# A folded block DFT, summed neighbour spectra and a list-scheduled program in a gated long-convolution and mixer kernel

## The chip, the cores and the metric

The kernel runs on one core of a Trainium2 chip. The metric is device time in microseconds (us) of that core, from the first instruction to the last. All data are bf16, with float32 sums in PSUM. A run counts as fast or slow by its time: a run that is over 1.5% above the fastest of the same kernel is called slow and is left out of the ratios.

Engine names in the profile: PE is TensorE's matmuls, PEld its weight loads, DVE is VectorE, ACT is ScalarE, POOL is GpSimd, SP is SyncE, which here only issues DMAs.

## The reference, cut to what matters

There are two branches over one sequence of 2048 rows of 640 channels, and a gate that mixes them. Branch A multiplies a 4-tap filter of `k` by `v`, convolves the product along the sequence with a filter as long as the sequence (`ssm_k`), and multiplies by `q`. Branch B is a mixer and an MLP with two layer norms.

```python
x = A_q                                            # (1, 2048, 640)
g = _sigmoid((x * gate_w).sum(-1, keepdims=True))
# branch A
for t in range(ks):                                # ks = 4
    k_shift = k_shift + k_pad[:, t:t + S, :] * shift_k[:, ks - 1 - t][None, None, :]
kv = k_shift * v
...
y_f = kv_f * kf_f[None, :, :, :]                   # FFTs of 4096: a causal convolution of 2048
y = y + kv * ssm_D[None, None, :]
a = q * y
# branch B
h = _gelu(_layernorm(x, axis=-1) @ w1)
# four groups of channels of h, shifted by +1, -1, +2, -2 rows
hs = jnp.concatenate([g0, g1, g2, g3], axis=-1) @ w2
x1 = x + hs
h2 = _gelu(_layernorm(x1, axis=-1) @ w3) @ w4      # w3 is 640x1536, w4 is 1536x640
b = x1 + h2
out = g * a + (1 - g) * b
```

I call the four products with `w1`, `w2`, `w3` and `w4` the first to fourth matmul, and the two layer norms LN1 and LN2.

## The kernel before

The convolution is done in four blocks of 512 rows by DFTs of 1024 points, as matmuls. The spectra of `kv` (per block) and of the filter (per block) are multiplied on VectorE, block by block, and summed. The frequencies and channels are cut into eight *units* (four groups of 128 frequencies times two halves of the channels). The inverse DFT is again matmuls; an output row needs the product spectra of its own block and of the block before it.

A helper records every operation with the names of what it reads and writes, and derives the waits. Each engine issues its operations in the order in which the program recorded them:

```python
    def _add(self, op):
        eng = op.eng
        op.ordinal = len(self.per_eng[eng])
        ...
        self.per_eng[eng].append(op)
        self.ops.append(op)
        return op
```

The product `kv` takes four shifted loads of `k` and eight operations of 640 elements for each tile of 128 rows:

```python
        for j in range(4):
            r0 = t * 128 - j
            if r0 >= 0:
                P.dma("sp", kvin[s][j], A_k[0, r0:r0 + 128, :], w=[("kvin", s, j)])
            ...
```

The second matmul's residual is added by VectorE as it reads PSUM, and VectorE also takes LN2's statistics:

```python
    def mm2_s1(t):
        ...
        P.op("dve", lambda e: e.tensor_tensor(
            x1t.rearrange("p (b n) -> p b n", b=2), ps2, xr.rearrange("p (b n) -> p b n", b=2), ALU.add),
             r=[("bankB", 2 * pr), ("bankB", 2 * pr + 1), ("xrel", t % 3)], w=[("x1rot", t % 3)])
        ...
        ln_act(1, t, x1t, ("x1rot", t % 3))
```

A unit multiplies block spectra in 30 VectorE operations, which cover the real and the imaginary part one by one:

```python
            else:
                for (ri_h, kvsel, ytgt, opc, un) in ((0, "re", "re", ALU.add, False), (1, "im", "re", ALU.subtract, False),
                                                      (0, "im", "im", ALU.add, useN), (1, "re", "im", ALU.add, False)):
                    ...
                    P.op(eng, lambda e, pt=pt, kvap=kvap, ri_h=ri_h, a=a, nbb=nbb, un=un: e.tensor_tensor(
                        pt[:, 0:nbb, :], kvap, Hbc(ri_h, a, nbb, n=un), ALU.mult), r=rk, w=[pk])
                    yap = Yre(a) if ytgt == "re" else Yim(a)
                    P.op(eng, lambda e, pt=pt, yap=yap, nbb=nbb, opc=opc: e.tensor_tensor(yap, yap, pt[:, 0:nbb, :], opc),
                         r=[pk, ykey], w=[ykey])
```

The inverse reads two blocks for each output tile, and the stages come one after the other:

```python
            for fcx in range(8):
                mm.append((fcx, c, 128 * q))
                if c >= 1:
                    mm.append((fcx, c - 1, 512 + 128 * q))
...
    for u in range(8):
        alloc_slots(u)
        fwd_dft("h", u)
        fwd_dft("kv", u)
        pointwise(u)
        release_slots(u)
...
    for sc in range(4):
        emit_mm3(sc)
        emit_mm4(sc)
...
    pipeline([inv_s0, inv_s1, inv_s2], NT)
```

## Time and profile before

Three runs took 500.69, 501.24 and 503.26 us, median 501.24. The profiled run had a span of 500.8 us.

| engine | busy us | share of the span |
|---|---|---|
| TensorE | 307.9 | 61% |
| VectorE | 270.7 | 54% |
| ScalarE | 177.2 | 35% |
| GpSimd | 28.6 | 6% |

No engine is near its limit over the whole span. The overview rows of the page show why: each character is one fortieth of the span (12.5 us), a digit is the busy share in tenths, PEclk is the clock that TensorE was granted in tenths, and DMA is the busy share of the 16 DMA engines. The trace has clock records from 117.0 us on only; the nines of PEclk before that stand for no record.

```profile
PE   1100000004993468999136750399899999999996
...
DVE  1666773872017767799999999667102020232122
...
PEclk9999999999799956999759975599999999999999
DMA  6399999980004564660000000002301010132221
```

Read the rows from left to right. First DMA is at 9 and TensorE is empty; then VectorE is at 9 while TensorE is partly empty; at the end TensorE is at 9 and VectorE is at 0 to 3. The same in numbers, from the view that sums the busy time of each engine over stretches. The first numbers are the stretch and its length; then come the busy times of PE, PEld, DVE, ACT and POOL with their instruction counts, the granted clock, the DMA share and GB/s.

```profile
0.00:125.00 125.00, 13.99 (x122) 7.24 (x123) 73.41 (x222) 56.25 (x155) 13.32 (x25) 1.00 0.86 196
125.00:145.00 20.00, 19.04 (x77) 8.26 (x79) 0.00 (x0) 15.87 (x29) 0.00 (x0) 0.86 0.00 0
145.00:206.00 61.00, 40.25 (x213) 21.64 (x211) 40.72 (x97) 8.33 (x16) 12.85 (x33) 0.83 0.48 119
206.00:346.00 140.00, 86.37 (x425) 43.72 (x425) 126.78 (x248) 53.72 (x101) 1.90 (x2) 0.80 0.10 33
346.00:435.00 89.00, 86.77 (x528) 51.76 (x532) 13.17 (x15) 30.38 (x49) 0.56 (x1) 1.00 0.16 52
435.00:501.00 66.00, 61.52 (x453) 44.09 (x451) 16.66 (x33) 12.69 (x16) 0.00 (x0) 0.99 0.24 75
```

The fourth row is the units: VectorE is busy 126.78 of 140 us, and TensorE works beside it at a clock of 0.80. The fifth is the third and fourth matmul, 86.77 of 89 us on TensorE with VectorE almost free. These are two long stages with different engines at their limit, and they run in turn. The third row, the second matmul, has neither engine full: the chain of waits shows there a loop of 3.67 us per tile (the residual add, two statistics, GpSimd's inverse root, the normalisation).

Two groups of instructions matter below, the inverse (L905) and the second matmul's residual add (L653). After the count come the busy time in us, the mean of one in ns, and the idle time of the engine before the group with what ended it.

```profile
L905 PE MATMUL PA<-arena 128*128 128x320 bf16 x448 | 61.0, 299 | 0.0
...
L653 DVE TENSOR_TENSOR arena<-PB,arena 128x640 bf16<-128x640 f32 x16 | 13.1, 818 | 23.0 <-PE PB L644 23.0
```

The residual add takes 818 ns on VectorE, and before it VectorE waits for TensorE, 23.0 us in all: it is a link of the loop, not a side job. A matmul of 320 columns shows 299 ns from start to end, but they overlap: 61.0 us for 448 is 136 ns each. The Trainium skill, page "TensorE: Matmul & The Clock Gate", section "Back-to-back issue gap", gives N/2.4 + 2.5 ns as the gap of an isolated matmul on a warm array, 135.8 ns for N = 320, and says that this over-counts for large N in a sustained stream, about 131 ns for N = 512. In the streams of this trace the median from one start to the next is 136 ns for 320 columns and 216 ns for 512: the formula (215.8 ns for 512) fits here, and the lower figure for a stream doesn't. Cadences like this one, not the mean durations, are what a count of matmuls is to be multiplied by.

### The profile page before, as it was taken

Reading aid. Unit: us, or ns where it says so; the run is one execution under the profiler, and the core shown is the slowest. Engines: PE = TensorE matmul, PEld = TensorE weight load, DVE = VectorE, ACT = ScalarE, POOL = GpSimd, SP = SyncE. Lnnn points to the kernel's source line nnn. Section 1 sums busy time; section 2 is a strip of 40 time slices with the busy share of each in tenths; the row PEclk is TensorE's granted clock in tenths of the full one; section 3 lists DMA queues with packets and bytes.
Section 4 is the critical chain, followed back from the end, with each engine's and each line's share of the span. In section 5 each row is a group of like instructions: output and inputs, shape, how many; then the busy total and the mean of one; then the engine's idle time right before and its main releaser. Section 6 shows DMA issues by size and latency. Waiting matters only on the chain.

```text
span 500.8 us, 5285 instructions
## 1 busy us (share of the span) xinstructions
PE 307.9 (61%) x1809; PEld 176.7 (35%) x1819; DVE 270.7 (54%) x612; ACT 177.2 (35%) x363; POOL 28.6 (6%) x60
## 2 busy tenths in 40 slices
PE   1100000004993468999136750399899999999996
PEld 0000000001352234555013320146455565777774
DVE  1666773872017767799999999667102020232122
ACT  1754443426760001776023320272433425021111
POOL 3210110000001221200000000000000000000000
PEclk9999999999799956999759975599999999999999
DMA  6399999980004564660000000002301010132221
GB/s 199 107 228 246 259 279 170 257 200 7 0 27 118 132 144 107 178 241 1 0 1 0 0 1 0 1 0 67 154 12 42 1 54 0 41 106 79 81 80 52
DMA packets 59113, 46.00 MB, mean 92 GB/s; under 512 B 35136, under 2 KB 57662, under 8 KB 58830
## 3 DMA queue, kind: packets, MB, share of 16 engines
q1 hardware_dynamic: 36062, 31.46, 23.6%
q10 hardware_dynamic: 21152, 5.25, 7.2%
q0 software_dynamic: 1872, 8.96, 5.2%
q8 instruction: 14, 0.23, 0.2%
q14 instruction: 13, 0.11, 0.1%
HBM read 32.54 MB, written 5.24 MB: 75 GB/s over the span
## 4 chain that ended last, share of the span: by engine, by line
DVE 40%; PE 31%; DMA 14%; ACT 4%; issue 4%; POOL 3%; SPq 2%; DVEq 0%; ACTq 0%; POOLq 0%
PE PA L905 12%; DVE arena L802 9%; DVE arena L799 8%; PE PB L845 8%; DMA arena<-in_A_k_dram 8%; PE PA L821 5%; PE PB L600 4%; DMA arena<-x_scratch 3%; DVE arena L653 3%; DMA arena<-in_A_v_dram 2%; POOL arena L506 2%; SPq L125 2%; DVE arena L498 2%; DVE arena L499 2%; PE PA L740 1%
## 5 line engine op out<-in xcount | busy, mean ns | idle before, releaser
L740 PE MATMUL PA<-arena 128*128 128x512 bf16 (+1 forms) x384 | 78.6, 371 | 53.5 <-ACT arena L743 53.5
L743 ACT ACTIVATE arena<-PA 128x512 bf16<-128x512 f32 (+1 forms) x96 | 50.5, 526 | 131.3 <-PE PA L740 65.9
L740 PEld LDWEIGHTS PA<-arena 128*128 128x128 bf16 x384 | 39.8, 105 | 92.2 <-ACT arena L743 56.6
L571 PE MATMUL PA<-arena 128*128 128x1 bf16 x80 | 4.7, 169 | 93.7 <-DMA arena<-arena 93.7
L905 PE MATMUL PA<-arena 128*128 128x320 bf16 x448 | 61.0, 299 | 0.0
L855 DVE SCALAR_TENSOR_TENSOR arena<-PB,arena 128x640 bf16<-128x640 f32 x16 | 14.1, 884 | 76.5 <-PE PB L845 73.3
L821 PE MATMUL PA<-arena 128*128 128x512 bf16 x232 | 51.9, 379 | 2.3 <-ACT arena L587 1.9
L845 PE MATMUL PB<-arena 128*128 128x320 bf16 x384 | 52.8, 299 | 0.0
L905 PEld LDWEIGHTS PA<-arena 128*128 128x128 bf16 x448 | 43.8, 98 | 17.0
L802 DVE TENSOR_TENSOR arena<-arena 128x960 bf16<-128x960 bf16 (+2 forms) x96 | 47.2, 492 | 3.3
L799 DVE TENSOR_TENSOR arena<-arena 128x960 bf16<-128x960 bf16 (+2 forms) x96 | 46.6, 485 | 0.0
L644 PE MATMUL PB<-arena 128*128 128x320 bf16 x160 | 31.1, 354 | 20.8 <-DVE arena L653 20.2
L845 PEld LDWEIGHTS PB<-arena 128*128 128x128 bf16 x384 | 37.6, 98 | 15.2
L571 PEld LDWEIGHTS PA<-arena 128*128 128x128 bf16 x80 | 3.4, 107 | 95.1 <-DMA arena<-arena 95.1
L821 PEld LDWEIGHTS PA<-arena 128*128 128x128 bf16 x240 | 23.3, 98 | 30.3 <-ACT arena L587 3.4
L920 DVE TENSOR_TENSOR arena<-arena 128x640 bf16<-128x640 bf16 x16 | 7.9, 493 | 45.5 <-ACT arena L914 45.5
L914 ACT ACTIVATE arena<-PA,arena 128x640 bf16<-128x640 f32 x16 | 12.7, 793 | 54.7 <-PE PA L905 54.7
L587 ACT ACTIVATE arena<-PA 128x512 bf16<-128x512 f32 x48 | 27.0, 595 | 14.0 <-PE PA L821 14.0
L807 ACT ACTIVATE arena<-arena 128x640 bf16<-128x640 bf16 x16 | 12.8, 824 | 46.6 <-DMA arena<-x_scratch 46.6
L600 PE MATMUL PB<-arena 128*128 128x512 bf16 x98 | 25.4, 425 | 6.3 <-ACT arena L587 6.0
L644 PEld LDWEIGHTS PB<-arena 128*128 128x128 bf16 x160 | 16.6, 111 | 35.2 <-DVE arena L653 26.0
L475 ACT ACTIVATE arena<-arena 128x640 bf16<-128x640 bf16 x16 | 11.8, 735 | 42.3 <-issue 18.9
(82 smaller groups left out, 285.6 us busy)
## 6 DMA issues: line engine op xcount, KB each, us to landing
arena<-in_A_k_dram SPq DMA_DIRECT2D x61, 160.0 KB, 6.3
arena<-in_A_q_dram SPq DMA_DIRECT2D x48, 160.0 KB, 2.5
arena<-in_B_w_dram POOLq DMA_DIRECT2D x2, 1920.0 KB, 12.8
arena<-in_A_v_dram SPq DMA_DIRECT2D x16, 160.0 KB, 7.2
x_scratch<-arena SPq DMA_DIRECT2D x16, 160.0 KB, 1.8
arena<-x_scratch SPq DMA_DIRECT2D x16, 160.0 KB, 2.2
out_dram<-arena SPq DMA_DIRECT2D x16, 160.0 KB, 1.8
arena<-cG POOLq DMA_DIRECT2D x1, 2048.0 KB, 8.4
```

The source lines that it names most:

```text
L587: P.op("act", lambda e, dst=dst, src=src: e.activation(dst, src, ACTF.Gelu_apprx_tanh), r=[key_ps], w=wk)
L600: P.op("pe", lambda e, lhsT=lhsT, c=c, sc=sc, psb=psb: e.matmul(psb, lhsT, xT[:, c, sc * 512:(sc + 1) * 512], start=(c == 0), stop=(c == D ...
L644: P.op("pe", lambda e, lhsT=lhsT, ft=ft, hh=hh, bk=bks[hh]: e.matmul(bk[:, 0:320], lhsT, w2v[:, ft, hh * 320:(hh + 1) * 320], start=(ft == ...
L653: P.op("dve", lambda e: e.tensor_tensor(x1t.rearrange("p (b n) -> p b n", b=2), ps2, xr.rearrange("p (b n) -> p b n", b=2), ALU.add), r=[( ...
L740: P.op("pe", lambda e, psb=psb, tc=tc, q0=q0, rhs=rhs, ncol=ncol: e.matmul(psb[:, 0:ncol], Rv[:, tc, q0:q0 + 128], rhs, start=(tc == 0), s ...
L743: P.op("act", lambda e, psb=psb, dst=dst, bb0=bb0, bb1=bb1, dd0=dd0, dd1=dd1, nb_=nb_, ncol=ncol: e.activation(dst[:, bb0:bb1, dd0:dd1], p ...
L799: P.op(eng, lambda e, pt=pt, kvap=kvap, ri_h=ri_h, a=a, nbb=nbb, un=un: e.tensor_tensor(pt[:, 0:nbb, :], kvap, Hbc(ri_h, a, nbb, n=un), AL ...
L802: P.op(eng, lambda e, pt=pt, yap=yap, nbb=nbb, opc=opc: e.tensor_tensor(yap, yap, pt[:, 0:nbb, :], opc), r=[pk, ykey], w=[ykey])
L821: P.op("pe", lambda e, psb=psb, c=c, ft=ft: e.matmul(psb, w3v[:, c, ft * 128:(ft + 1) * 128], xT[:, c, sc * 512:(sc + 1) * 512], start=(c ...
L845: P.op("pe", lambda e, bk=bk, fcx=fcx, tt=tt, hh=hh: e.matmul(bk[:, 0:320], uT[:, fcx, (tt % 4) * 128:(tt % 4) * 128 + 128], w4v[:, fcx, h ...
L855: P.op("dve", lambda e: e.scalar_tensor_tensor(out=Bp[:, tt, :].rearrange("p (b n) -> p b n", b=2), in0=ps2, scalar=gcol(tt, 1), in1=x1r.r ...
L905: P.op("pe", lambda e, bk=bk, fcx=fcx, cc=cc, u0=u0, hh=hh, i=i, n_mm=n_mm: e.matmul(bk[:, 0:320], Gv[:, fcx, u0:u0 + 128], Yv[:, fcx, cc, ...
```

## The change

The intent is to give TensorE less to do, to give VectorE fewer and larger operations, and above all to let a scheduler put the stages beside each other. The parts are:

1. The DFT is taken at half-offset points, so that cosine and sine rows are even and odd about the middle of a block. A block is first folded (first half plus and minus the reversed second half), which halves the rows that the forward matmuls contract over.
2. The spectra of neighbouring blocks are summed per frequency before the units (`combine`), so that the inverse needs one block, not two.
3. A unit takes 19 operations, with the real and imaginary parts in one access pattern.
4. `kv` is made from one load with five rows per partition and one product of 5120 elements.
5. The residuals of second and fourth matmul are added on TensorE by a matmul with the identity; LN2's sums come from ScalarE's accumulator, and six small GpSimd operations make the mean and the inverse root of them.
6. The helper tracks hazards by memory region, and a list scheduler with constants for the cost of each operation orders the whole program for all engines before it is emitted. All transposes and nearly all loads and stores are issued by SyncE.

The diff, cut to its core (of some 850 lines on each side; `...` marks cuts):

```diff
-        self.per_eng[eng].append(op)
...
+    def schedule(self, bw=250.0, tbw=90.0, dlat=1900.0, lat=90.0, backlog=2500.0):
...
+                for i in cand[e]:
+                    st = max(f, ready[i])
+                    if ops[i].nbytes and not ops[i].tp:
+                        st = max(st, dfree - backlog)
+                    key = (st, -(ops[i].rank + ops[i].bias), i)
+                    if pick is None or key < pick:
+                        pick = key
...
-        P.op("dve", lambda e: e.tensor_tensor(pA, k0, SHK[0], ALU.mult), r=[("kvin", s, 0), ("SHK", 0)], w=[("ktmp", s, 0)])
...
+            P.dma(sp, kt, bass.AP(A_k.tensor, A_k.offset + (t0 - 3) * D, [[2 * D, 128], [D, 5], [1, D]]))
...
+        tt(kpr, win, SHK.unsqueeze(1).to_broadcast([128, 2, 4, 640]), ALU.mult)
...
+            tt(o, k[:, :, 0:256].rearrange("p b (n s) -> p b s n", s=2),
+               k[:, :, 511:255:-1].rearrange("p b (n s) -> p b s n", s=2), op)
...
-        P.op("dve", lambda e: e.tensor_tensor(
-            x1t.rearrange("p (b n) -> p b n", b=2), ps2, xr.rearrange("p (b n) -> p b n", b=2), ALU.add),
...
+            pairs.append((ident, xr[t % 3][:, hs]))
+            mm(pr[:, h, :], pairs)
+        act(x1[t % 3].rearrange("p (b n) -> p b n", b=2), pr, ACTF.Copy, accum=st[1, 0][:, t:t + 1])
+        act(xn2[t % 3], x1[t % 3], ACTF.Square, accum=st[1, 1][:, t:t + 1])
...
+        ts(s[2], s[0], 1.0 / D, None, ALU.mult, eng="pool")
+        ts(s[3], s[1], 1.0 / D, 1e-5, ALU.mult, ALU.add, eng="pool")
+        tt(s[4], s[2], s[2], ALU.mult, eng="pool")
+        tt(s[3], s[3], s[4], ALU.subtract, eng="pool")
...
+    def combine(b):
+        tt(XF[:, b, 0:2], XF[:, b, 0:2], XF[:, b - 1, 0:2], ALU.add)
+        tt(XF[:, b, 2:4], XF[:, b, 2:4], XF[:, b - 1, 2:4], ALU.subtract)
...
-                mm.append((fcx, c, 128 * q))
-                if c >= 1:
-                    mm.append((fcx, c - 1, 512 + 128 * q))
+        pairs = [(G[:, j, r, 128 * q:128 * (q + 1)], slots[order.index((j, hh))][:, r, c, :]) for j in range(4) for r in range(2)]
...
+    for i in range(4):
+        at(3, unit, i)
+    for sc in range(1, 4):
+        mm3(sc)
+        for i in range(4):
+            mm4(4 * sc + i)
+    for i in range(4, 8):
+        at(3, unit, i)
...
+    sched = P.schedule()
     with nc.Block() as block:
+        P.emit(block, sched)
```

## The prediction

It was written before the changed kernel ran.

> **What bounds the kernel now.** A row of stages (windows view). 0-125 us: loads, LN1, kv; DMA row at 9, VectorE 73 us busy. 145-206: second matmul in a VectorE loop of 3.67 us per tile (chain). 206-345: pointwise units; VectorE 99% full, 15.9 us for each of eight units of 30 operations; TensorE 40-60% busy at clock 0.6-0.8. 346-497: TensorE alone, 99% busy, clock 1.0: four rounds of third (8.8 us) and fourth matmul (13.05 us), then the inverse, 448 matmuls in 60.9 us. VectorE is mostly idle there.
>
> **What changes, in the trace's cadences** (TensorE 216 ns per 512 columns, 136 per 320).
> - TensorE: neighbour spectra are summed first, so the inverse is 256 matmuls, not 448 (-26 us); folding takes the forward from 256x512 plus 128x256 to 80x512 plus 144x320. Identity matmuls for residuals add 64x320 (+9). In all about 229 us at full clock, was 278.
> - VectorE: a unit keeps its 23,040 elements in 19 operations: about 13.7 us for 15.9. kv products become 32 large operations (46 us) plus folds (6); neighbour sums add 8.6. LN1 statistics come over from ScalarE (19); LN2 statistics and two residual adds leave (-50). The filter's folds read with step 2. The Trainium skill, "VectorE: DVE Perf Modes", section "What auto-detection actually checks", asks step 1 for the double rate, so I estimate 1.2 us for each of ten; nothing here shows it. Sum about 235 us, was 271.
> - ScalarE about 165 us, was 177. k is read 2.5 times in 6.4 KB rows, not 4 times in 1.3 KB rows.
> - Mainly order: the instruction order puts the units beside second, third and fourth matmul. Two stages that ran in turn (139 us VectorE, 150 us TensorE) overlap.
>
> **Sum.** Front: VectorE 99 us, DMA about as long, first tap rows at about 16 us: VectorE done with it at 120, the first MLP matmul at 105. Then TensorE has second 26, third 52, fourth 57, inverse 35 = 170 us. The second is bound by ScalarE (1.9 us per tile) and three buffers: 50 us including leftovers and the first third-matmul round. Then 131 us at 98%: 105 + 55 + 135 + tail 5 = 300. VectorE, 120 + 117 + stalls, ends just before; its order leaves 14 of 16 output pairs to the end, behind TensorE. I add a little for in-order stalls: the scheduler's constant for a 640-wide eviction, 660 ns, is under the measured 793.
>
> **Predicted 307 us**, 8 in 10 between 283 and 340. Faster by over 2%: 0.97; within: 0.02; slower: 0.01. All on the chain: about 25 front, 40 second matmul, 139 hidden, 25 inverse, less 35 of lost overlap.
>
> **What would show it.** Right: VectorE and TensorE each over 75% of the span; last 130 us TensorE at 9 and clock 1.0; a unit near 13.7 us; filter folds 1.1-1.3 us; the chain ends in 320-wide matmuls. Wrong: units still running after the last fourth matmul (then VectorE bounds); second-matmul tiles over 3 us.
>
> **What could make it wrong.** (1) LN2's six small GpSimd operations per tile now run beside two-input VectorE operations; the skill, "GPSIMD Engine Reference", section "1. Specifications", says the SBUF interfaces are shared and contend. Before, they took 222 and 568 ns with VectorE mostly waiting, so the trace cannot show it. A microsecond's wait each would make the second matmul 70 us: about 330. (2) Every transpose and load is on one in-order queue; one late producer blocks the rest. (3) Low clock in the front.

## The result, and the profile after

The changed kernel's median is 308.13 us (fast runs 306.93, 306.96 and 309.31; one run of 312.00 was slow; a fifth, 313.01, which the median leaves out, was slow too). In the same rounds the kernel before had a median of 500.97. The ratio is 0.615, with a 95% interval of 0.6086 to 0.6215. A ratio here is the mean time of one kernel's fast runs over that of the other's of the same rounds, so it is not quite the ratio of the medians quoted. The prediction was 307, so the total was right. The question for the experiments is whether it was right for the stated reasons.

The overview of the profiled run (a fast one, span 307.5 us), in slices of 7.7 us:

```profile
PE 249.3 (81%) x1526; PEld 144.0 (47%) x1526; DVE 229.0 (74%) x352; ACT 151.5 (49%) x289; POOL 87.8 (29%) x156
...
PE   0401949876797998747899599999999999999994
...
DVE  4489997989983934948879999999999991121343
...
PEclk9999997996999999887999799999999999999999
DMA  7978999978934047996633630004101311023342
```

TensorE and VectorE now have their nines in the same slices. The stretches, in the same columns as before:

```profile
0.00:100.00 100.00, 60.05 (x330) 26.91 (x331) 80.04 (x125) 55.12 (x102) 31.59 (x53) 0.95 0.87 226
100.00:179.00 79.00, 64.80 (x384) 37.92 (x383) 60.74 (x85) 47.66 (x104) 54.53 (x100) 0.94 0.61 165
179.00:257.00 78.00, 78.00 (x487) 46.94 (x486) 75.38 (x118) 29.06 (x49) 1.67 (x4) 1.00 0.17 43
257.00:308.00 51.00, 46.41 (x331) 32.18 (x329) 12.80 (x26) 19.61 (x35) 0.00 (x0) 0.98 0.28 78
```

In the third row both engines are over 95% busy at a clock of 1.00. This is what the change was for. The second row is not so good: TensorE 64.80 of 79 us, VectorE 60.74 of 79. The end of the chain of waits (start, duration, what) says what ended last:

```profile
178.80 124.63 PE PSall L506 x816
303.45 0.54 ACT arena L498
304.01 0.50 DVE arena L488
304.54 0.49 DVE arena L488
```

From 178.80 us on, 816 matmuls run without a break; one eviction, two VectorE operations and a store follow. The prediction had given the stages their own times, so they can be laid side by side. The first MLP matmul is over when its last 512-column matmul ends, ahead of a long run of 320-column ones; that is between 104.4 and 104.8 us.

| stage | predicted us | measured us |
|---|---|---|
| until the end of the first MLP matmul | 105 | about 104.6 |
| from there until TensorE runs without a break | 55 | 74.2 (178.8 - 104.6) |
| TensorE without a break | 135 | 124.6 |
| tail | 5 | 4.1 (307.5 - 303.4) |
| allowed for stalls in order | 7 | - |
| sum | 307 | 307.5 |

The middle stage was 19 us longer than its own line (the prediction's text has 50 us for it, its sum 55). The 7 us allowed for stalls and a last stage that was 10 us shorter made up for it. Two things shortened the last stage. The prediction's 135 us leave 4 us over its 131 us of matmuls for stalls, and there were none. And TensorE had done more of the later work: after 178.8 us, 170 matmuls of 512 columns and 646 of 320 remain, where the prediction's 131 us left 180 and 672 (three rounds of the third, all of the fourth, the inverse). The 10 and 26 that were pulled forward are 10 x 216 + 26 x 136 ns, 5.7 us.

How TensorE spent the middle stage (the same view, for this stretch alone):

```profile
104.60:178.80 74.20, 60.02 (x357) 35.80 (x356) 55.94 (x81) 44.81 (x100) 53.42 (x98) 0.93 0.65 176
```

It was busy for 60.0 us and idle for 14.2. So this stage would have been over its 55 us without a single wait. Its matmuls (286 of 320 columns and 70 of 512) come to 54 us at the cadences above, an estimate: second matmul 26, one round of the third 13, 9 for 67 forward-transform matmuls that were still left, and the 5.7 pulled forward. The other 6 us are slower matmuls, at a granted clock of 0.93 in the mean.

The VectorE groups that answer to the prediction's costs:

```profile
L488 DVE TENSOR_TENSOR arena<-arena 128x1280 bf16<-128x1280 bf16 x66 | 52.2, 817 | 5.2 <-PE PSall L506 4.0 <-ACT arena L498 0.9
L488 DVE TENSOR_TENSOR arena<-arena 128x2560 bf16<-128x2560 bf16 x28 | 41.6, 1485 | 3.2 <-ACT arena L498 3.0
...
L488 DVE TENSOR_TENSOR arena<-arena 128x5120 bf16<-128x5120 bf16 x8 | 22.6, 2824 | 3.1 <-ACT arena L498 2.8
...
L488 DVE TENSOR_TENSOR arena<-arena 128x1024 bf16<-128x1024 bf16 x10 | 11.8, 1210 | 0.0
```

The last line is the filter's folds with step 2: 1024 elements take 1210 ns, longer than 1280 elements with step 1 in the first line (817 ns). The prediction's estimate was 1.2 us.

### The profile page after: what moved, and what is told of

It reads as the page before. It is cut to its first block, busy times and chain, and to the rows that moved or that the text cites. A ratio compares the mean times of both kernels' runs of the same rounds, so it can differ in the third digit from the quotient of the medians.

```text
span 307.5 us, 4162 instructions
## 1 busy us (share of the span) xinstructions
PE 249.3 (81%) x1526; PEld 144.0 (47%) x1526; DVE 229.0 (74%) x352; ACT 151.5 (49%) x289; POOL 87.8 (29%) x156
## 3 DMA queue, kind: packets, MB, share of 16 engines
q1 hardware_dynamic: 52848, 35.40, 44.8%
## 4 chain that ended last, share of the span: by engine, by line
PE 52%; DVE 21%; DMA 11%; POOL 8%; ACT 4%; issue 3%; SPq 0%; ACTq 0%; POOLq 0%
PE PSall L506 51%; DVE arena L488 16%; DMA arena<-arena 8%; ACT arena L498 4%; POOL arena L652 3%; DVE arena L645 2%; POOL arena L488 2%; DMA arena<-in_A_shift_k_dram 2%; POOL arena L493 2%; DMA arena<-in_A_ssm_k_dram 2%; DVE arena L493 1%; POOL arena L661 1%; POOL arena L156 1%; DVE arena L646 1%; SPq L153 0%
## 5 line engine op out<-in xcount | busy, mean ns | idle before, releaser
L506 PE MATMUL PSall<-arena 128*128 128x320 bf16 (+3 forms) x1521 | 248.6, 323 | 46.2 <-ACT arena L498 14.2
L488 DVE TENSOR_TENSOR arena<-arena 128x640 bf16<-128x640 bf16 (+8 forms) x253 | 199.1, 836 | 51.0 <-ACT arena L498 43.4
L506 PEld LDWEIGHTS PSall<-arena 128*128 128x128 bf16 (+1 forms) x1521 | 143.5, 100 | 151.1 <-issue 32.5
L498 ACT ACTIVATE arena<-PSall 128x512 bf16<-128x512 f32 (+4 forms) x190 | 109.0, 613 | 85.6 <-PE PSall L506 68.5
L498 ACT ACTIVATE arena<-PSall,arena 128x320 bf16<-128x320 f32 (+1 forms) x48 | 29.5, 616 | 56.0 <-PE PSall L506 52.9
L493 POOL TENSOR_SCALAR arena<-arena 128x1 f32<-128x1 f32 (+2 forms) x44 | 23.0, 524 | 74.9 <-DVE arena L646 55.7
L493 DVE TENSOR_SCALAR arena<-arena 128x640 bf16<-128x640 bf16 (+2 forms) x36 | 15.5, 450 | 20.6 <-POOL arena L488 20.3
L488 POOL TENSOR_TENSOR arena<-arena 128x1 f32<-128x1 f32 (+2 forms) x60 | 24.4, 411 | 12.6 <-DVE arena L493 8.9
L645 DVE BATCH_NORM_STATS2 arena<-arena 128x6 f32<-128x320 bf16 x32 | 13.8, 473 | 3.0 <-DMA arena<-in_A_q_dram 3.0
L661 POOL TENSOR_TENSOR arena<-arena 128x1 f32<-128x1 f32 x16 | 12.9, 804 | 1.1
```

The lines of the kernel that those rows point to most:

```text
L488: P.op(eng, lambda e: e.tensor_tensor(o, a, b, op), [a, b], [o], dve_ns(o, [a, b], 2) if eng == "dve" else 250)
L493: P.op(eng, lambda e: e.tensor_scalar(o, a, s1, s2, op0=op0, **({} if op1 is None else {"op1": op1})), [a] + aps, [o], dve_ns(o, [a], 3) + ...
L498: P.op("act", lambda e: e.activation(o, a, f, bias=bias, scale=scale, **({"accum_out": accum} if accum is not None else {})), [a] + aps, [ ...
L506: fns.append(lambda e, l=l, r=r, i=i: e.matmul(o, l, r, start=(i == 0), stop=(i == len(pairs) - 1)))
L645: P.op("dve", lambda e, o=o, i=i: e.bn_stats(o, i), [i], [o], 420)
L661: P.op("pool", lambda e: e.tensor_tensor(s[5], s[3], neghalf[:, t0:t1], ALU.pow), [s[3], neghalf[:, t0:t1]], [s[5]], 600)
```

## The experiments

Twelve kernels ran, in four sets; within a set all ran on the same chip beside the kernel before, whose median was 500.9 to 502.1 us. Where the text says "order frozen", each engine keeps the changed kernel's order of instructions, so that only the stated edit differs. "The control" is the changed kernel once more.

| run | median us | lowest to highest | ratio to before (95%) |
|---|---|---|---|
| changed kernel | 308.13 | 306.93 to 312.00 | 0.6150 (0.6086 to 0.6215) |
| e11 control | 308.58 | 307.69 to 309.16 | 0.6167 (0.6126 to 0.6208) |
| e1 units before the second matmul | 415.69 | 414.99 to 417.58 | 0.8290 (0.8211 to 0.8369) |
| e2 recorded order | 605.54 | 604.49 to 607.00 | 1.2060 (1.1967 to 1.2152) |
| e3 two-block inverse | 337.39 | 334.86 to 339.44 | 0.6716 (0.6647 to 0.6785) |
| e4 forward matmuls twice | 324.68 | 324.22 to 324.85 | 0.6464 (0.6415 to 0.6512) |
| e5 LN2's small operations on VectorE | 314.70 | 312.26 to 317.62 | 0.6304 (0.6259 to 0.6349) |
| e6 more GpSimd operations in LN2 | 311.40 | 311.12 to 311.80 | 0.6219 (0.6204 to 0.6234) |
| e7 folds with step 1 | 310.43 | 309.24 to 311.32 | 0.6198 (0.6176 to 0.6219) |
| e8 fourth residual on VectorE | 306.25 | 304.12 to 308.03 | 0.6114 (0.6081 to 0.6147) |
| e9 four buffers in the second matmul | 319.36 | 317.51 to 320.39 | 0.6376 (0.6319 to 0.6433) |
| e10 folds with step 1 and less of k loaded | 307.11 | 303.36 to 311.54 | 0.6114 (0.6049 to 0.6179) |
| e12 less of w3 and w4 loaded | 307.21 | 305.92 to 310.41 | 0.6147 (0.6115 to 0.6178) |

All but e12 passed the comparison with the reference; e10 computes with missing rows of `k`, and the comparison's tolerance doesn't see it, presumably because the convolution's part of the output is small with these inputs (not tested). The medians of the changed kernel and its control differ by 0.45 us and their runs spread over 2 to 3 us, so I call nothing under 2 us a difference. Differences in the text below are taken from 308.4 us, the middle of these two medians. Medians and ranges count every run, slow ones too: 312.00 of the changed kernel, 317.62 of e5 and 311.54 of e10. The seven fast runs of changed kernel and control have a median of 308.27 us, so this matters for e5 and e10 only. (The ratio for e5 counts its slow run.)

### e1: is the gain the overlap?

The theory is that most of the gain is VectorE's units running beside second, third and fourth matmul. The edit tells the helper, falsely, that the first tile of the second matmul reads all unit outputs, so the units must come first; nothing is removed or added.

```diff
-            mm(pr[:, h, :], pairs)
+            mm(pr[:, h, :], pairs, after=list(slots[0:8]) if t == 0 else ())
...
+    for i in range(8):
+        at(3, unit, i)
     for t in range(12):
         mid(t)
```

> The changed kernel with one false dependence: the first group of the second matmul also waits for all eight pointwise units, so the units run before it instead of beside it (the units are recorded ahead of it). Result correct. Theory (the overlap of the units with the second, third and fourth matmul is the largest part of the gain): units from about 124 to 241 us, then second matmul about 40, then 131 and a tail of 5: 405 to 425 us, that is 100 or more lost. Rival (most of the gain is less work on each engine and the overlap is worth little because the engines slow each other down): under 345 us.

It took 415.69 us, 107 us more. The stretches show the stages in turn again, VectorE 114.72 of 122 us alone and then TensorE 118.84 of 123 us alone:

```profile
110.00:232.00 122.00, 12.50 (x62) 5.20 (x62) 114.72 (x171) 7.53 (x13) 4.26 (x8) 0.56 0.08 21
232.00:290.00 58.00, 52.30 (x321) 31.17 (x323) 7.79 (x19) 33.54 (x80) 25.75 (x100) 0.98 0.71 167
290.00:413.00 123.00, 118.84 (x775) 75.62 (x778) 15.75 (x32) 47.90 (x82) 0.00 (x0) 0.99 0.20 55
```

The theory holds, and so does its size: the prediction's "139 hidden, less 35 of lost overlap" is 104. One thing blurs the number: this kernel was scheduled anew, and the new order pushed the last five matmuls of the first MLP matmul behind the units (TensorE waited 97.86 us for a small VectorE copy that stood behind them, and then ran five 512-column matmuls, 2.3 us), so the 107 is not the overlap alone. A sign of the idle time is the clock row of the page, where TensorE is granted half its clock while the units run. The Trainium skill, page "TensorE: Matmul & The Clock Gate", section "What's actually happening", has the clock at half rate after idling, and here it stands at 5 tenths in the slices in which TensorE is idle:

```profile
PE   1136757888816000000000677999999999999996
...
PEclk9997999898977555555555699999999999999999
```

The units could be timed here without other work beside them: the last four took 57.9 us, 14.5 us each, where the prediction had 13.7 and the kernel before 15.93.

### e2: what is the scheduler worth?

The same operations, hazards and buffers, in the order in which the program records them.

```diff
-    sched = P.schedule()
+    for n_, o_ in enumerate(P.ops):
+        o_.order = n_
+    sched = P.ops
```

> The changed kernel without its list scheduler: every engine issues in the order in which the program records its operations, dependences unchanged. Result correct. Theory A (the recorded order already has units beside matmuls, but prefetch and the LN2 loop need the scheduler): about 370, range 340 to 410. Theory B (the author's interleaving does it all): under 320. Theory C (all the overlap comes from the scheduler): over 410.

It took 605.54 us: my own expectation of 340 to 410 was far off, and the rival of over 410 held. Without the scheduler the new program is 21% slower than the kernel before. The timeline shows the mechanism (SPq is the issue on SyncE; the bracket is the idle time before and what ended it):

```profile
256.28 0.45 DVE L493 TENSOR_SCALAR arena<-arena 128x640 bf16<-128x640 bf16 x1 [18.13 <-POOL arena L488]
256.75 1.20 SPq L153 DMA_TRANSPOSE arena<-arena  x1
258.00 0.58 SPq L156 DMA_DIRECT2D arena<-in_A_q_dram  x1
...
260.41 2.05 PE L506 MATMUL PSall<-arena 128*128 128x320 bf16 x7 [7.59 <-DMA arena<-in_A_q_dram]
```

A load of the residual that needs nothing from VectorE stands in SyncE's order behind a transpose that waits for VectorE. When VectorE has written its 640 elements, the transpose goes out, then the load, then TensorE starts. TensorE waited 116.7 us in 14 such places; each time the load had gone out right behind a transpose. That is 117 of the 297 us lost; the rest was not taken apart. So the scheduler is not a polish on top of the other parts: without it they lose. The run shows that this recorded order is bad; an order placed by hand, as the kernel before has it, was not tried with the new parts.

### e3: the summed neighbour spectra

The sums are taken out again and the inverse reads two blocks (448 matmuls, and a half-sized negated matrix, since two of the groups need the other sign).

```diff
-    for b in (3, 2, 1):
-        at(2, combine, b)
...
+        if c >= 1:
+            pairs += [((G if j < 2 else GN)[:, j if j < 2 else j - 2, r, 128 * q:128 * (q + 1)],
+                       slots[order.index((j, hh))][:, r, c - 1, :]) for j in range(4) for r in range(2)]
```

> Undoes one part: no sums of neighbouring spectra on VectorE (six operations of 2560, about 8.6 us); the inverse takes both blocks, 448 matmuls of 320 instead of 256, with a second, negated half of the inverse matrix. Result correct. Theory (TensorE bounds the last 125 us): plus 192 x 136 ns = 26 us, about 334, range 328 to 340. Rival (VectorE or evictions bound the tail): under 318.

It took 337.39 us, 29 us more. 192 matmuls at 136 ns are 26.1 us, so the whole TensorE time of the second block comes through, even though VectorE's 8.3 us less (229.0 to 220.7 us busy) would have been a gain. It holds: the last stage is bound by TensorE, and a matmul saved there is a matmul's time saved. This run was scheduled anew, so some of the 3 us may be the order.

### e4: the folded forward

Each forward matmul is issued twice (the first pass into the same PSUM bank, overwritten by the second), which gives back about the TensorE work that folding took away; order frozen.

```diff
+        if twice:
+            for i, (l, r) in enumerate(pairs):
+                fns.append(lambda e, l=l, r=r, i=i: e.matmul(o, l, r, start=(i == 0), stop=(i == len(pairs) - 1)))
```

> Every forward-transform matmul (80 of 512 and 128 of 320) is issued twice, the second overwriting the first, about as much TensorE work as before folding; all engines' orders unchanged. Result correct. Theory (VectorE paces the first 95 us and TensorE has slack there, so folding's TensorE saving is mostly off the chain): 308 to 322. Rival (TensorE paces the front): plus 35, about 343.

It took 324.68 us, 16 us more for 35 us of added matmuls (80 x 216 + 128 x 136 ns). The theory's 308 to 322 was missed by 3 us, and the rival's 343 by far more. About half of the work is paid for. The other half disappears in TensorE's idle time in the front (in the first 90 us TensorE was busy 59.86 us, for 51.78 in the changed kernel) and in a higher granted clock (0.984 for 0.965), so this is not a clean dose. Folding is therefore worth something, but less than its matmuls.

### e5 and e6: do GpSimd's small operations set the pace of the second matmul?

The middle stage was the step that missed its time. Its tiles follow each other in 4.4 us: the normalisations of tiles 0 to 11 start between 110.92 and 159.29 us, 48.4 us for 11 steps (the first and the last of them):

```profile
110.92 0.45 DVE L493 TENSOR_SCALAR arena<-arena 128x640 bf16<-128x640 bf16 x1 [2.96 <-POOL arena L488]
...
159.29 0.45 DVE L493 TENSOR_SCALAR arena<-arena 128x640 bf16<-128x640 bf16 x1 [1.00 <-POOL arena L488]
```

TensorE was busy for 38.3 of these 48.4 us, 3.5 us per tile, where a tile's own twelve matmuls take 1.6 (12 x 136 ns): most of the pitch is other work that the order puts between the tiles. The experiments below ask about the rest, the waits.

The prediction had 1.9 us; before it was 3.67, and in e1, without units beside them, the same normalisations went from 239.67 to 268.12 us, 2.6 us each. The groups of GpSimd, in the changed kernel from 130 to 180 us:

```profile
L493 POOL TENSOR_SCALAR arena<-arena 128x1 f32<-128x1 f32 x21 | 15.1, 720 | 9.3 <-ACT arena L498 8.5
L488 POOL TENSOR_TENSOR arena<-arena 128x1 f32<-128x1 f32 x31 | 13.0, 426 | 1.7
L661 POOL TENSOR_TENSOR arena<-arena 128x1 f32<-128x1 f32 x11 | 9.9, 900 | 0.7
```

and in e1 from 236 to 290 us, where VectorE is nearly idle:

```profile
L661 POOL TENSOR_TENSOR arena<-arena 128x1 f32<-128x1 f32 x16 | 9.2, 577 | 1.1
L488 POOL TENSOR_TENSOR arena<-arena 128x1 f32<-128x1 f32 x48 | 9.0, 196 | 2.8
L493 POOL TENSOR_SCALAR arena<-arena 128x1 f32<-128x1 f32 x32 | 6.8, 213 | 23.0 <-ACT arena L498 22.7
```

The same operations on one element per partition take 213, 196 and 577 ns alone, and 720, 426 and 900 ns beside the units. One of them took 4.23 us, at 144.97, while VectorE was in a row of twelve two-input operations (144.35 to 151.71). The Trainium skill, page "GPSIMD Engine Reference", section "1. Specifications", says that GpSimd's SBUF interfaces are shared with VectorE and that they contend with VectorE instructions that have two SBUF inputs. The traces agree with that and give the size.

It doesn't follow that the time hangs on it. e5 moves five of the six operations to VectorE (the inverse root stays; order frozen):

```diff
-        ts(s[2], s[0], 1.0 / D, None, ALU.mult, eng="pool")
-        ts(s[3], s[1], 1.0 / D, 1e-5, ALU.mult, ALU.add, eng="pool")
-        tt(s[4], s[2], s[2], ALU.mult, eng="pool")
-        tt(s[3], s[3], s[4], ALU.subtract, eng="pool")
+        ts(s[2], s[0], 1.0 / D, None, ALU.mult)
+        tt(s[4], s[2], s[2], ALU.mult)
+        P.op("dve", lambda e: e.scalar_tensor_tensor(out=s[3], in0=s[1], scalar=1.0 / D, in1=s[4], op0=ALU.mult, op1=ALU.subtract),
+             [s[1], s[4]], [s[3]], 70)
+        ts(s[3], s[3], 1e-5, None, ALU.add)
```

> LN2's small statistics arithmetic: five of its six operations per tile move from GpSimd to VectorE, only the power stays on GpSimd; the schedule is the changed kernel's, operation for operation. Result correct. Theory (GpSimd's waits beside VectorE sit in the loop of the second matmul and delay TensorE): 297 to 304. Rival A (transposes and the three buffers pace that loop, GpSimd is hidden): 306 to 310. Rival B (VectorE in order now waits for ScalarE and GpSimd and delays the units): 312 or more.

GpSimd's busy time fell from 87.8 to 51.3 us, and the kernel became slower: 314.70 us, 6 us more, or 5 by its fast runs (312.26, 313.09 and 316.31). The theory had 297 to 304; rival B had this. VectorE does these operations only when its fixed order reaches them, and then it stands still until their input is there: from 100 to 190 us it waited 5.6 us for ScalarE ahead of the first of them and 4.1 us for the inverse root, with the units behind it. In the changed kernel it waited 13.8 us for GpSimd from 100 to 180 us, so the waits did get shorter, but VectorE had 8.1 us more to do (237.1 for 229.0 us busy). The matmul that begins TensorE's unbroken run at 178.80 us in the changed kernel started at 181.03 in e5.

e6 goes the other way: 64 more GpSimd operations in LN2 with no use of their results, one ahead of four of the six in each tile. Each is tied to its operation as one item, so the schedule stays as it was.

```diff
+        n0 = len(P.ops)
         ln_math(1, t0, t1)
+        for k_ in (0, 1, 2, 4):
+            d_ = dummy[:, t0 * 4 + min(k_, 3):t0 * 4 + min(k_, 3) + 1]
+            P.ops[n0 + k_].fns = [lambda e, d_=d_: e.tensor_scalar(d_, neghalf[:, 0:1], 1.0, None, op0=ALU.mult)] + P.ops[n0 + k_].fns
```

> Four more small GpSimd operations per tile in LN2 (64 in all), each ahead of one of the six real ones, writing to spare columns; schedule unchanged. Result correct. Theory (GpSimd's chain paces the second matmul): plus 8 to 25 us. Rival (hidden): under plus 3.

GpSimd's busy time rose from 87.8 to 111.3 us in all; the time rose by 3 us, to 311.40, at the edge of the rival's range and far from the theory's. Each added operation stands in the chain of its tile, so if the middle stage were paced by this chain alone, the added time of its twelve tiles, 18 us of the 23.5, would have come out. So the contention is real, and GpSimd's chain alone doesn't pace the stage. What the contention costs is not measured: e5 took most of these operations away, but put waits on VectorE in their place.

### e7 and e10: the front

e7 folds the filter with step 1 (a second, reordered copy of the forward matrix makes the result the same):

```diff
-            tt(o, k[:, :, 0:256].rearrange("p b (n s) -> p b s n", s=2),
-               k[:, :, 511:255:-1].rearrange("p b (n s) -> p b s n", s=2), op)
+            tt(o, k[:, :, 0:256].rearrange("p b (s n) -> p b s n", s=2),
+               k[:, :, 511:255:-1].rearrange("p b (s n) -> p b s n", s=2), op)
```

> The filter's ten even/odd folds read and write with step 1 (the halves of the block are split in place of even and odd rows, with their own copy of the forward matrix, 512 KB more to load); schedule unchanged. Result correct. Theory (step 2 costs the double rate, and VectorE paces the front): folds 1.21 to about 0.6 us each and 4 to 6 us less in all, about 303. Rival A (the reversed operand costs it too): folds stay at 1.2, time unchanged. Rival B (folds get faster but the front is not paced by VectorE): folds 0.6, time within 2 us.

```profile
L490 DVE TENSOR_TENSOR arena<-arena 128x1024 bf16<-128x1024 bf16 x10 | 6.5, 675 | 0.0
```

The fold fell from 1210 to 675 ns: the Trainium skill, page "VectorE: DVE Perf Modes", section "What auto-detection actually checks", asks a step of +1 or -1 on every 16-bit tensor for the double rate, and the run agrees, also with one operand read backwards. VectorE's busy time fell by 5.2 us (229.0 to 223.8). The time did not fall: 310.43 us, as rival B had it. VectorE waited longer for DMA in its place (6.2 us for row loads in the first 100 us, 3.0 in the changed kernel; one of these waits is 4.11 us long) and for TensorE (6.9 us for 4.0). The extra matrix of 0.5 MB that this edit needs is a confound, as it loads the DMA that VectorE then waits for.

e10 adds to e7 that five of the eight loads of `k` fetch two rows of each five only, 2.5 MB less (so their products are wrong):

```diff
+            if u < 2:
+                P.dma(sp, kt, bass.AP(A_k.tensor, A_k.offset + (t0 - 3) * D, [[2 * D, 128], [D, 5], [1, D]]))
+            else:
+                P.dma(sp, kt[:, 3:5, :], bass.AP(A_k.tensor, A_k.offset + t0 * D, [[2 * D, 128], [D, 2], [1, D]]))
+                P.ops[-1].nbytes = 819200
```

> The step-1 folds of e7 and, besides, five of the eight loads of k fetch two rows per partition instead of five (2.5 MB less; the other three rows keep old data, so the result is wrong on purpose); schedule kept. Theory (with faster folds the front waits for DMA, which moved about 256 GB/s there at full share, so 2.5 MB are up to 9 us): 300 to 306. Rival (neither VectorE nor DMA volume paces the front, but latency of the in-order queue and of dependences): 308 to 311.

It took 307.11 us (303.36 to 311.54). That is between both expectations, no difference from the control by my rule, and the widest spread of all; its three fast runs give the ratio of e8, 0.6114. Its profile fell into the slow run of 311.54 us, so I draw nothing from it beyond a hint: in it the front ended 2.6 us earlier and TensorE then stood still for 9.81 us in the middle stage. If that is typical, the middle stage absorbs what the front saves; fast runs would have to show it.

### e8: the residual of the fourth matmul

VectorE adds it again, so 32 identity matmuls go:

```diff
-            mm(pr[:, h, :], [(uT[:, c, 128 * i:128 * (i + 1)], w4[:, c, hs]) for c in range(FC)] + [(ident, x1r[t % 3][:, hs])])
+            mm(pr[:, h, :], [(uT[:, c, 128 * i:128 * (i + 1)], w4[:, c, hs]) for c in range(FC)])
```

> Undoes half of one part: the fourth matmul's residual is added by VectorE from SBUF (16 operations of 640) and no longer by an identity matmul (32 matmuls of 320 less). Result correct. Theory (TensorE bounds the last 125 us and VectorE has slack): minus 32 x 136 ns = 4.4 us, about 304. Rival (the extra VectorE work, in order between units, delays the inverse): 308 or more.

TensorE's busy time fell by 5.4 us (249.3 to 243.9), VectorE's rose by 12.0 (to 241.0), and the median is 306.25, 2 us less, between the theory's 304 and the rival's 308. This run was scheduled anew, so the order may have a share in it. Its ratio, 0.6114 (0.6081 to 0.6147), overlaps those of the changed kernel and the control. The direction fits a last stage that is bound by TensorE; it is no version that beats the changed kernel for sure.

### e9: a fourth buffer for the second matmul

Residual, result and normalised tile get four buffers, in space that the first matmul's weights leave free; order frozen.

```diff
-    x1 = [V(oX1 + 640 * i, 640) for i in range(3)]
+    x1 = [V(o, 640) for o in (oX1, oX1 + 640, oX1 + 1280, oWA + 640)]
```

> Four buffers instead of three for the residual rows, the sums and the normalized rows of the second matmul (the fourth lies in space that the first matmul's weights have left); schedule kept. Result correct. Theory (the loop of ScalarE, GpSimd, VectorE and transpose over three buffers makes TensorE idle in the second matmul): 299 to 305. Rival (static order and the latency from one stage to the next, not the buffer count): within 2 us of the changed kernel.

It took 319.36 us, 11 us more. One wait says why:

```profile
PE PSall L506 <- DMA arena<-cG: 11.0, 1, 11.0
```

The space was wanted for the inverse matrix too, whose load was now issued at 212.3 us and not at 170.4, and TensorE waited 11.0 us for it. Without that wait the run would be 319.4 - 11.0 = 308.4 us, an estimate that leaves nothing for the fourth buffer. But the wait also left TensorE at half its clock until 221.4 us, and just before it e9 was ahead: up to the place where the two orders of matmuls part (the edit shifted a few), TensorE was 3.0 us early, 187.5 for 190.5 us, though e9's front had ended 1.1 us later. So neither expectation was met, the edit had a side effect that I should have seen, and it stays open whether the fourth buffer is worth some 2 to 4 us (an estimate from one profiled run each); it isn't worth the 14.

### e11 and e12: the control, and the DMA load of the middle stage

> The changed kernel once more, unaltered, to say how far its own runs spread: all theories expect 306 to 312.

The control's 308.58 us against 308.13 shows what a repeat is worth.

The last suspect for the middle stage was the load of `w3` and `w4` (3.9 MB) that is in flight there; TensorE's waits of 2.20 and 1.14 us for a residual's load fit it. e12 loads 0.69 MB of it, with a wrong result (relative error 16.6); order frozen.

```diff
-    P.dma("pool", w3, B_w3.rearrange("(c p) f -> p c f", p=128))
+    P.dma("pool", w3[:, 0:1, :], B_w3.rearrange("(c p) f -> p c f", p=128)[:, 0:1, :])
+    P.ops[-1].nbytes = 1966080
```

> The two loads of the third and fourth matmul's weights fetch 0.38 and 0.31 MB instead of 1.97 MB each (the rest of the tiles keeps old data, so the result is wrong on purpose); same orders on all engines. Theory (these 3.9 MB, which can start only when the front has left their space, fall into the second matmul, slow its transposes and residual loads and cost TensorE about 9 us of idle time between 125 and 150 us): 298 to 304, the transposes there back to about 3 us each. Rival (the idle time is the latency of the LN2 chain in a static order, GpSimd included): 306 to 310, the same holes in TensorE.

It took 307.21 us over six runs, 0.6147 of before, where my theory had 298 to 304 and the rival 306 to 310. TensorE was idle 7.5 us of the 25 from 125 to 150 us, for 9.0 in the changed kernel. What SyncE did in that stretch of e12:

```profile
126.03 6.87 SPq L153 DMA_TRANSPOSE arena<-arena  x2
132.94 0.58 SPq L156 DMA_DIRECT2D arena<-in_A_q_dram  x1
```

Two transposes hold the queue for 6.87 us: 1.2 us each to issue, and 4.4 us in which the second waits for its input, which VectorE writes late (at 131.20, after 1.58 us of waiting for GpSimd). The residual's load goes out behind them at 132.94, and TensorE resumes at 135.5 after 5.49 us of idling. TensorE's gaps in the changed kernel (the bracket is the idle time before):

```profile
128.85 5.07 PE L506 MATMUL PSall<-arena 128*128 128x320 bf16 x24 [2.20 <-DMA arena<-in_A_q_dram]
138.82 3.18 PE L506 MATMUL PSall<-arena 128*128 128x320 bf16 x12 [4.91 <-ACT arena L498]
143.15 4.13 PE L506 MATMUL PSall<-arena 128*128 128x320 bf16 x22 [1.14 <-DMA arena<-in_A_q_dram]
```

So the long wait in e12, which the profile puts down to a DMA, was not one for bandwidth, but for a place in the queue. The changed kernel's gap of 1.14 us has the same shape: its load went out behind a transpose at 140.40 and landed at 143.10. The gap of 2.20 us has not: its load went out at 122.31 and landed only at 128.71, and in e12, with few weights in flight, the gap there is 0.72 us. So the weights may cost some 1.5 us there, an estimate from one profiled run each (the control has 1.82). No run moved the residual's loads to another engine's queue, so whether that alone would help is open.

## Why the prediction was right or wrong

**The total and the main mechanism: right.** 307 predicted, 308.13 measured. The hidden time of 104 us net is 107 by e1. The last stage is TensorE at 9 with a clock of 1.00, as predicted, and the chain ends in 320-column matmuls. Of the 193 us gained, e1 and e3 account for 107 and 29; for the rest, the front and the second matmul, no run isolates a cause.

**The inverse: right.** 26 us of matmuls were predicted to go (25 in the sum), and e3 gives 29.

**The costs on VectorE: nearly right.** Folds 1.21 us for 1.2, all of VectorE 229.0 for 235, the neighbour sums done at 124 us for 120. A unit took 14.5 us (e1) and not 13.7. VectorE over 75% of the span was named as a sign; it is 74%, a miss in a sign, with no effect on the time. ScalarE's 165 us was too high by 13.5 (151.5).

**The front: right in its time, partly untested in its cause.** The first MLP matmul was to end at 105 us and ended at 104.6. e7 shows that taking 5 us from VectorE alone gives nothing; e4 shows that adding 35 us of matmuls costs about half of it. So the front is not paced by VectorE alone or by TensorE alone; the runs don't say more. The split "25 front, 40 second matmul" has no run that isolates it.

**The step that failed: "The second is bound by ScalarE (1.9 us per tile) and three buffers: 50 us".** The tiles took 4.4 us, the "over 3 us" that the prediction itself had named as a sign of being wrong, and the stage 74 us instead of 55 with its leftovers. ScalarE's cost was right: its four operations per tile take 702 + 201 + 738 + 195 ns, 1.84 us. But it was not the bound: in the 74.2 us of the stage ScalarE was busy 44.8 us and TensorE 60.0, 15 of these with leftovers of the forward transform and matmuls pulled forward, 6 with a lower clock; 14.2 us were waits. Reason (1) under what could go wrong, GpSimd beside two-input VectorE operations, did happen, and it was to make 330 us of it. It didn't, for two reasons. GpSimd's chain isn't what paces the stage alone: 18 us more in it cost 3 (e6). And the last stage gave back 10 of the 19 us, 5.7 of them because TensorE had already done part of the third and fourth matmul in the middle stage. The 7 us allowed for stalls took up nearly all of the rest. A sum of stages puts work into the wrong line when a scheduler is free to pull later work forward. So the total was right partly by luck: an error of 19 us in one line met a margin and a gain elsewhere.

**What sets the 4.4 us is settled in part.** TensorE's own work takes 3.5 us of it. What paces the rest is not settled. The chain of a tile goes from TensorE to ScalarE, to GpSimd, to VectorE, to a transpose, each in a fixed order with the units' operations in between; without the units it takes 2.6 us (e1). Three suspects were tried one at a time, GpSimd's share (e5, e6), the buffers (e9) and the weights' DMA (e12), and none gave back more than a few of the 14.2 us that TensorE stands still between 117.8 and 178.8 us (15.1 in the control). Either it is the order itself, with all of them a little late, or the place of loads behind transposes in one queue (reason (2) of the prediction, which e2 shows in its extreme form and e12 in a mild one). To tell these apart would take a run with the loads on another queue and a run with a schedule made from measured durations.

No version that was run beats the changed kernel beyond the spread.

## What to carry to other kernels

When two stages of one kernel have different engines at their limit, what is to be had is at most the shorter of the two (here 139 us, of which 35 were expected to be lost), and it can be checked by adding one false dependence that puts them in turn again (here 107 us of the 193 gained). An order made by a scheduler is part of such a change and not a finish on it: the same operations in the program's own order took 605 us, and 117 us of this TensorE waited for independent loads that stood behind transposes. A suspicious wait in a trace, even one with a true mechanism behind it, should be doubled or removed in a run before anybody works on it, and the idle time of the engine that bounds the stage says first what there is to gain (14 us here); here none of the four that were removed or moved (e5, e7, e9, e12) gained more than the spread, and two of them cost time.

## What the Trainium skill lacked or had wrong

- "GPSIMD Engine Reference", section "1. Specifications", states the contention with two-input VectorE instructions without a size ("SBUF — State Buffer", section "Who interferes with whom", mentions one measurement of 1.5 times, without its operations). Here operations on 128x1 float32 took 196, 213 and 577 ns with VectorE nearly idle, 426, 720 and 900 ns in the mean beside the units (1.6 to 3.4 times), and up to 4.23 us.
- "DMA: Bandwidth & Descriptors", section "Issuing engines are not separate DMA queues", counts only the sequencer's issue time as what a second issuing engine saves. Here a load without any dependence on it stood behind a transpose that waited 4.4 us for its input on the same issuing engine (e12), and in e2 TensorE lost 116.7 us in 14 waits for loads that went out right behind a transpose. Whether a second issuing engine would save this was not run.
- "VectorE: DVE Perf Modes", section "Side-by-side: where the cycles go for N=2048 bf16", lists one size. Its breakdown at the double rate, (N/2 + 8 + 150) cycles at 0.96 GHz, gives 498, 831, 1498 and 2831 ns for 640, 1280, 2560 and 5120 elements; the means here are 486, 817, 1485 and 2824 ns, so it may be used at these sizes (within 3%).
- "TensorE: Matmul & The Clock Gate", section "Back-to-back issue gap", has about 131 ns per matmul of 512 columns in a sustained stream and calls 216 ns over-counted. Here the median in unbroken streams is 216 ns, before and after the change.
